# Loading k and v with four tokens on each of 128 partitions and the last 64 tokens apart

## The chip, the core and the metric

The kernel runs on one core of one Trainium2 chip. The metric is the device time of one execution in microseconds (us), as the median of several runs. A core has TensorE (PE, with PEld for its weight loads), VectorE (DVE), ScalarE (ACT), GpSimd (POOL) and SyncE (SP), and 16 DMA engines that move data between the device memory (HBM) and the on-chip memory (SBUF, 128 partitions). In this kernel SP issues every DMA, on one queue.

## The reference, cut to what matters

Inputs q, k and v have the shape (4, 8, 576, 64): batch, heads, tokens, head size, in float32. The first stage is an attention without softmax, the second and third are two feed-forward stages over the 2304 tokens.

```python
kv = np.einsum('bhsd,bhse->bhde', k, v)          # 64 x 64 for each batch and head: a sum over the 576 tokens
out = np.einsum('bhsd,bhde->bhse', q, kv)
x = out / np.sqrt(np.mean(out * out, axis=-1, keepdims=True) + 1e-06) * g_norm
x = x.transpose(0, 2, 1, 3).reshape(2304, 512)
h = np.maximum(np.maximum(x @ w1, x @ w2), x @ w3)
x = h @ w_out                                    # the first feed-forward stage
for e in range(4):                               # the second one, with p the normalized domain_probs
    y += p[:, e:e + 1] * (np.maximum(x @ e_w1[e], 0) @ e_w2[e])
```

The sum over tokens in kv may be taken in any order, as long as k and v put the same token in the same place.

## The kernel before, in words

All matrix products are done by PE in float32 or in split float32. The kernel has three stages, whose instructions are written out in one order for all engines; each engine takes its own in that order and waits for what an instruction needs.

The attention stage reads a string of steps (`steps`, from line 680). `K b c` (`att_kv`, line 261) forms kv of two heads of batch b from the tiles of k and v; each tile holds four heads, so the tile pair (b, c) serves `K b 2c` and `K b 2c+1`. Per head there are five products, one for each column i of the tile: four sum over 128 partitions, the last over the first 64. After the fourth K step of a batch, ACT copies kv into a padded operand (`kvb`). `T` (`att_T`) transposes a tile of q (line 297), `O` (`att_O`) multiplies it by kvb (lines 313 and 321) and squares the outcome (line 334), `N` (`att_N`) normalizes it on DVE, `X` (`att_X`) transposes it for the next stage (line 364, with a copy at 368 or 370). Between them stand the steps `a` and `b` (`conv_a`, `conv0`, `conv1`), which turn the weights of the first feed-forward stage from 64-bit words into float32 on ACT, POOL and DVE (lines 199 to 211), and `A`, `H`, `P`, the first products of that stage (lines 249 and 415). The steps end near 135 us in the profile; the two feed-forward stages follow, with the products at lines 537 and 577 as the bulk of the time.

The loads of q, k, v and of these weights are issued by SP in the order of the list `order` (line 637): k00 q0 k01 q1 q2 k10 k11 q3 q4 q6 k20 q5 k21 k30 k31, then three weight tiles, q8, q9 and further weights; each "k" entry is a call of `load_kv` and loads a tile of k and one of v. There are buffers for six tiles of k and v (three pairs) and six of q. `pump` emits the loads as far as buffers have been released by the steps emitted so far, and on the chip SP waits for that release.

A tile of k or v has 128 partitions, four heads, five columns and 64 values. In the kernel before, partitions 0 to 63 get five successive tokens each (tokens 0 to 319), partitions 64 to 127 four each (tokens 320 to 575), by one DMA for each half: 64 partitions x 4 heads packets of 1280 and of 1024 bytes. Tiles of q take two tokens for each partition and head, so packets of 512 bytes; the tile of the last 64 tokens of all batches (q2) comes as four DMAs of 32 partitions.

Of the kernel before, what the change touches and what calls it, by code (L numbers as in the profile page):

```python
# [21 lines left out]
def tile_attn_moe_moe2(  # L22
# [23 lines left out]
    nc = tc.nc  # L46
    B, H, S, D = q.shape
# [3 lines left out]
    P = 128  # L51
# [8 lines left out]
    KC = S // P  # L60
# [56 lines left out]
    for b0 in range(0, B, 2):  # L117
        for b, s0 in ((b0, 0), (b0, 256), (b0, None), (b0 + 1, 0), (b0 + 1, 256)):
# [3 lines left out]
            else:  # L122
                rows = out[b * S + s0 : b * S + s0 + 256, :].rearrange("(p r) d -> r p d", r=2)
# [20 lines left out]


    HALF = P // 2
    KS = HALF * (KC + 1)

    def load_kv(pool, b, c):
        for src, nm in ((k, "k"), (v, "v")):  # L150
            t = pool.tile([P, 4, KC + 1, D], F32, tag="kv", name=f"{nm}{b}_{c}", bufs=6)
            rows = src[b, 4 * c : 4 * c + 4]
            nc.sync.dma_start(out=t[0:HALF], in_=rows[:, 0:KS, :].rearrange("h (p c) d -> p h c d", c=KC + 1))
            nc.sync.dma_start(
                out=t[HALF:P, :, 0:KC, :], in_=rows[:, KS:S, :].rearrange("h (p c) d -> p h c d", c=KC)
            )
            kv_sb[nm, b, c] = t


# [246 lines left out]
    def moe1_h(pool, j, f, xs):  # L406
        for i in range(3):
            moe1_a(i, j, f, xs)
        return moe1_split(pool, j, f)
# [210 lines left out]
    with tc.manual_schedule():  # L620
# [114 lines left out]
        h = moe1_h(None, 2, 0, xs)  # L735
# [12 lines left out]
        for j in range(2, NB):  # L748
            acc = new_acc(KD)
            for f in range(NF):  # L750
                if j > 2 or f:
                    h = moe1_h(None, j, f, xs)
# [117 lines left out]
```

## Time and profile before

| | |
|---|---|
| median of 3 runs | 1159.07 us (1158.97 to 1159.13) |
| the profiled execution | 1160.35 us, span 1158.5 us |
| PE busy | 1123.4 us (97%) |
| PEld, the weight loads, beside PE | 1033.8 us (89%) |
| DVE busy | 562.4 us (49%) |
| ACT busy | 391.1 us (34%) |
| POOL busy | 238.1 us (21%) |
| DMA on the queue of SP | 98.62 MB in 73824 packets, 28.0% of the 16 engines' span |

The span runs from the first to the last instruction of the profiled execution; the rest of its time lies around that. A busy share is the mean over stages with different limits. A row of a timeline gives the start, the duration, the engine, the line in the kernel, the operation with what it writes and reads, and in brackets the idle time before it and what ended that; neighbouring instructions of one kind are merged. A DMA issue has a time to landing, from the start of its issue on SP until its data has arrived. A transfer's packet is one contiguous piece.

### The profile page before, as it was taken

The numbers are of one execution on the slowest core, as the hardware profiler recorded it, in microseconds if no ns is written. First come the engines' busy times: TensorE is split into PE (matmuls) and PEld (weight loads), VectorE is DVE, ScalarE is ACT, GpSimd is POOL, SyncE is SP. The second block draws the span as 40 slices with busy tenths as digits, with TensorE's granted clock in tenths as the row PEclk, the third lists the DMA queues.
The fourth block names the chain that finished last, engine by engine and source line by source line (L and its number), as shares of the span: only waits on it lengthen the run. The fifth ranks groups of instructions, "written<-read, shape, count | busy, mean of one in ns | idle before, by whom it ended". The sixth has DMA issues, their size and how long they took to land.

```text
span 1158.5 us, 15032 instructions
## 1 busy us (share of the span) xinstructions
PE 1123.4 (97%) x6096; PEld 1033.8 (89%) x6096; DVE 562.4 (49%) x842; ACT 391.1 (34%) x699; POOL 238.1 (21%) x178
## 2 busy tenths in 40 slices
PE   5699899999999999999999999999999999999998
PEld 5689799999999988888888888888888888888887
DVE  0689982221315544343753435583534666453523
ACT  2463331121214434243553233352323253332321
POOL 1156760000300130205220110512020522002000
PEclk9899999999999999999999999999999999999999
DMA  9963421000201220204250403424040625030111
GB/s 206 226 169 109 146 74 56 2 28 1 64 1 65 68 87 28 82 7 157 65 191 1 160 4 114 141 74 145 19 146 1 216 66 191 1 130 35 46 64 55
DMA packets 73894, 99.59 MB, mean 86 GB/s; under 512 B 6240, under 2 KB 49248, under 8 KB 73824
## 3 DMA queue, kind: packets, MB, share of 16 engines
q1 hardware_dynamic: 73824, 98.62, 28.0%
q8 instruction: 48, 0.79, 0.3%
q14 instruction: 22, 0.18, 0.0%
HBM read 75.01 MB, written 23.59 MB: 85 GB/s over the span
## 4 chain that ended last, share of the span: by engine, by line
PE 87%; DVE 5%; DMA 4%; SPq 2%; ACT 1%; issue 1%; POOL 1%; DVEq 0%; ACTq 0%
PE bank L577 35%; PE bank L537 30%; PE bank L249 15%; PE bank L415 6%; DMA k<-in_k_dram 2%; DMA stage_a<-in_moe_w_dram 1%; DVE cv_a L208 1%; DMA v<-in_v_dram 1%; DVE cv_a L211 1%; SPq L135 1%; DVE cv_a L207 0%; DVE fa L394 0%; PE bank L297 0%; SPq L611 0%; POOL cv_o L200 0%
## 5 line engine op out<-in xcount | busy, mean ns | idle before, releaser
L577 PE MATMUL bank<-wr,hr 128*128 128x512 f32 x792 | 227.1, 395 | 0.0
L561 DVE TENSOR_TENSOR fa<-bank,fa 128x384 f32<-128x384 f32 x144 | 80.2, 557 | 214.1 <-ACT fa L558 120.4
L577 PEld LDWEIGHTS bank<-wr,hr 128*128 128x128 f32 x792 | 147.0, 188 | 20.7
L519 POOL TENSOR_TENSOR fa<-fa 128x768 f32<-128x768 f32 x48 | 97.1, 2033 | 299.4 <-DMA fa<-y_d 221.6
L249 PE MATMUL bank<-xr,wr 128*128 128x384 f32 x792 | 145.2, 340 | 5.8 <-DVE fa L394 2.5
L249 PEld LDWEIGHTS bank<-xr,wr 128*128 128x128 f32 x792 | 139.6, 188 | 8.7 <-DVE fa L394 3.4
L488 POOL TENSOR_TENSOR w1s<-w1s 128x256 f32<-128x256 f32 x64 | 55.7, 890 | 421.6 <-DMA w1s<-in_moe_w_dram 420.4
L558 ACT ACTIVATE fa<-bank 128x384 f32<-128x384 f32 x144 | 70.7, 491 | 194.5 <-PE bank L537 194.5
L537 PE MATMUL bank<-rb,wr 128*128 128x384 f32 x648 | 131.6, 338 | 0.3 <-DVE hr L545 0.3
L537 PE MATMUL bank<-xr,wr 128*128 128x384 f32 x648 | 131.6, 338 | 0.0
L537 PEld LDWEIGHTS bank<-rb,wr 128*128 128x128 f32 x648 | 116.6, 188 | 10.2 <-DVE hr L545 0.6
L537 PEld LDWEIGHTS bank<-xr,wr 128*128 128x128 f32 x648 | 116.7, 188 | 9.6
L577 PE MATMUL bank<-wr,xr 128*128 128x512 f32 x324 | 100.8, 396 | 0.0
L394 DVE TENSOR_TENSOR fa<-bank,fa 128x384 f32<-128x384 f32 x72 | 39.8, 555 | 117.7 <-PE bank L249 117.5
L249 PE MATMUL bank<-xr,wl 128*128 128x384 f32 x504 | 90.5, 335 | 0.0
L249 PEld LDWEIGHTS bank<-xr,wl 128*128 128x128 f32 x504 | 87.4, 188 | 0.2 <-DVE wl L185 0.2
L577 PE MATMUL bank<-wl,hr 128*128 128x512 f32 x288 | 86.3, 394 | 0.0
L545 DVE SCALAR_TENSOR_TENSOR hr<-fa,hr 128x384 fp32r<-128x384 f32 x72 | 49.7, 690 | 42.6 <-ACT hr L544 42.6
L577 PEld LDWEIGHTS bank<-wr,xr 128*128 128x128 f32 x324 | 60.7, 188 | 10.8
L544 ACT ACTIVATE hr<-fa 128x384 fp32r<-128x384 f32 x72 | 37.8, 525 | 77.1 <-DVE fa L561 77.1
L577 PEld LDWEIGHTS bank<-wl,hr 128*128 128x128 f32 x288 | 53.4, 188 | 7.0
L544 ACT ACTIVATE xr<-fa 128x384 fp32r<-128x384 f32 x48 | 25.2, 525 | 96.7 <-DVE fa L561 96.7
(132 smaller groups left out, 1481.9 us busy)
## 6 DMA issues: line engine op xcount, KB each, us to landing
fa<-y_d SPq DMA_DIRECT2D x22, 768.0 KB, 6.4
stage_a<-in_moe_w_dram SPq DMA_DIRECT2D x18, 512.0 KB, 3.6
o_d<-fa SPq DMA_DIRECT2D x36, 256.0 KB, 3.7
fa<-o_d SPq DMA_DIRECT2D x36, 256.0 KB, 5.6
w1s<-in_moe_w_dram SPq DMA_DIRECT2D x32, 256.0 KB, 3.2
w2s<-in_moe_w_dram SPq DMA_DIRECT2D x32, 256.0 KB, 4.1
y_d<-fa SPq DMA_DIRECT2D x6, 768.0 KB, 3.8
o_d<-ob SPq DMA_DIRECT2D x18, 256.0 KB, 2.0
```

The source lines that it names most:

```text
L135: nc.sync.dma_start(out=t[bb * n : (bb + 1) * n], in_=q[bb, :, SB:S, :].rearrange("h (p r) d -> p h r d", r=2))
L249: nc.tensor.matmul(ps, w[:, wi, c * P : (c + 1) * P], x[xi][:, c, :], start=(n == 0), stop=(n == 3 * KD - 1),)
L394: nc.vector.tensor_tensor(out=ms[j, f], in0=ps[:, :T], in1=ms[j, f], op=ALU.max)
L415: nc.tensor.matmul(acc[c][:, :T], w[:, wi, c * P : (c + 1) * P], h[hi], start=(f == 0 and n == 0), stop=(f == NF - 1 and n == 2),)
L488: eng.tensor_tensor(out=st[:, o], in0=st[:, a], in1=st[:, b], op=ALU.subtract)
L519: eng.tensor_tensor(out=yb[:, o], in0=yb[:, a], in1=yb[:, b], op=op)
L537: nc.tensor.matmul(out, w[wi][:, c * P : (c + 1) * P], y[yi][:, c, :], start=(i == 0 and k in BEGIN), stop=(i == 5), skip_group_check=k no ...
L544: nc.scalar.activation(out=h[0], in_=src, func=AF.Relu)
L545: nc.vector.scalar_tensor_tensor(out=h[1], in0=src, scalar=0.0, in1=f32(h[0]), op0=ALU.max, op1=ALU.subtract)
L558: nc.scalar.activation(out=s[k // 2], in_=a, func=AF.Copy)
L561: nc.vector.tensor_tensor(out=t, in0=x, in1=t, op=ALU.add)
L577: nc.tensor.matmul(banks[i], h[a, i // TPB][hi][:, i % TPB * P : (i % TPB + 1) * P], w[a][wi], start=(pr == 0 and a == 0 and m == 0), stop ...
```

## The change

A tile keeps its shape, and the products are as before. The first DMA now fills all 128 partitions with four successive tokens each (tokens 0 to 511, `KS = P * KC`), 128 partitions x 4 heads packets of 1024 bytes. The second fills the fifth column of partitions 0 to 63 with one token each (tokens 512 to 575), 64 partitions x 4 heads packets of 256 bytes.

```diff
     HALF = P // 2
-    KS = HALF * (KC + 1)
+    KS = P * KC

     def load_kv(pool, b, c):
         for src, nm in ((k, "k"), (v, "v")):
             t = pool.tile([P, 4, KC + 1, D], F32, tag="kv", name=f"{nm}{b}_{c}", bufs=6)
             rows = src[b, 4 * c : 4 * c + 4]
-            nc.sync.dma_start(out=t[0:HALF], in_=rows[:, 0:KS, :].rearrange("h (p c) d -> p h c d", c=KC + 1))
-            nc.sync.dma_start(
-                out=t[HALF:P, :, 0:KC, :], in_=rows[:, KS:S, :].rearrange("h (p c) d -> p h c d", c=KC)
-            )
+            nc.sync.dma_start(out=t[:, :, 0:KC, :], in_=rows[:, 0:KS, :].rearrange("h (p c) d -> p h c d", c=KC))
+            nc.sync.dma_start(out=t[0:HALF, :, KC, :], in_=rows[:, KS:S, :].rearrange("h p d -> p h d"))
             kv_sb[nm, b, c] = t
```

## Rows read from the trace of the kernel before

**Rows 1.** The page, part 4: the chain that ended last, shares of the span by line.

```profile
PE bank L577 35%; PE bank L537 30%; PE bank L249 15%; PE bank L415 6%; DMA k<-in_k_dram 2%; DMA stage_a<-in_moe_w_dram 1%; DVE cv_a L208 1%; DMA v<-in_v_dram 1%; DVE cv_a L211 1%; SPq L135 1%; DVE cv_a L207 0%; DVE fa L394 0%; PE bank L297 0%; SPq L611 0%; POOL cv_o L200 0%
```

**Rows 2.** Stretches: width, busy us by engine, granted PE clock, DMA share, GB/s.

```profile
0.00:64.00 64.00, 42.66 (x461) 38.38 (x462) 24.46 (x54) 25.18 (x51) 12.10 (x13) 0.95 1.10 218
...
75.00:135.00 60.00, 56.40 (x334) 53.15 (x332) 57.67 (x93) 24.12 (x46) 40.03 (x28) 1.00 0.37 115
135.00:1158.00 1023.00, 1015.77 (x5205) 935.46 (x5204) 472.61 (x681) 333.91 (x588) 181.78 (x135) 1.00 0.22 75
```

**Rows 3.** The timeline of PE, 0 to 75 us.

```profile
9.04 1.53 PE L271 MATMUL bank<-v,k 128*64 128x64 f32 x20 [9.04 <-DMA v<-in_v_dram]
...
33.15 2.55 PE L271 MATMUL bank<-v,k 128*64 128x64 f32 x40 [3.84 <-DMA v<-in_v_dram]
...
48.02 1.09 PE L297 MATMUL bank<-ident,q 128*128 128x128 f32 x8 [2.03 <-DMA q<-in_q_dram]
...
53.46 2.41 PE L271 MATMUL bank<-v,k 128*64 128x64 f32 x40 [3.47 <-DMA v<-in_v_dram]
...
66.29 0.66 PE L364 MATMUL bank<-ident,xt 128*128 128x128 f32 x4 [0.22 <-DVE fa L370]
66.88 1.82 PE L271 MATMUL bank<-v,k 128*64 128x64 f32 x40
70.94 1.56 PE L297 MATMUL bank<-ident,q 128*128 128x128 f32 x8 [2.24 <-ACT s L344]
```

**Rows 4.** The timeline of SP's DMA issues, 42 to 66 us.

```profile
42.69 1.10 SPq L154 DMA_DIRECT2D v<-in_v_dram  x1
...
53.34 0.59 SPq L154 DMA_DIRECT2D v<-in_v_dram  x1
...
58.99 6.58 SPq L139 DMA_DIRECT2D q<-in_q_dram  x2
```

**Rows 5.** The DMA issued from 59 to 59.5 us: KB, us to landing.

```profile
q<-in_q_dram SPq DMA_DIRECT2D x1, 512.0 KB, 11.8
```

**Rows 6.** Stretches in which one kind of load moves (columns as in rows 2).

```profile
18.00:20.00 2.00, 2.00 (x24) 1.76 (x23) 0.00 (x0) 0.54 (x2) 0.00 (x0) 1.00 1.20 200
33.00:36.00 3.00, 2.85 (x42) 2.47 (x43) 1.95 (x6) 0.20 (x1) 0.00 (x0) 0.64 1.21 290
37.00:39.00 2.00, 2.00 (x24) 1.61 (x23) 0.69 (x1) 1.40 (x3) 0.00 (x0) 0.94 1.12 197
58.00:63.00 5.00, 5.00 (x59) 4.69 (x57) 3.92 (x4) 3.78 (x9) 3.16 (x1) 1.00 1.11 220
64.00:66.00 2.00, 2.00 (x30) 1.53 (x28) 1.90 (x4) 0.26 (x1) 0.00 (x0) 1.00 1.10 346
```

**Rows 7.** The second DMA of v21, issued from 42.6 to 42.8 us.

```profile
v<-in_v_dram SPq DMA_DIRECT2D x1, 256.0 KB, 10.6
```

**Rows 8.** The second DMA of v31, among those issued from 50 to 55 us.

```profile
v<-in_v_dram SPq DMA_DIRECT2D x1, 256.0 KB, 11.1
```

**Rows 9.** The timeline of SP, 200 to 420 us: the loads of p_all.

```profile
201.54 2.02 SPq L611 DMA_DIRECT2D p_all<-in_moe_domain_probs_dram  x4
```

**Rows 10.** The page, part 6: DMA issues, KB each, median us to landing.

```profile
p_all<-in_moe_domain_probs_dram SPq DMA_DIRECT2D x8, 4.0 KB, 1.9
```

**Rows 11.** Waits of SP's queue, 0 to 90 us: total, times, longest us.

```profile
SPq L154 <- DMA q<-in_q_dram: 2.9, 2, 2.0
SPq L153 <- DMA k<-in_k_dram: 1.8, 2, 0.9
```

**Rows 12.** The page, part 2: all DMA packets.

```profile
DMA packets 73894, 99.59 MB, mean 86 GB/s; under 512 B 6240, under 2 KB 49248, under 8 KB 73824
```

**Rows 13.** The timeline of ACT: the first conversion of a weight tile.

```profile
65.74 0.66 ACT L199 ACTIVATE cv_a<-stage_a 128x512 f32<-128x512 f32 x1 [2.22 <-DMA stage_a<-in_moe_w_dram]
```

**Rows 14.** The timeline of DVE, 58 to 76 us.

```profile
58.80 0.96 DVE L70 CAST xr<-fa 128x1536 fp32r<-128x1536 f32 x1 [5.71 <-ACT fa L368]
...
75.08 0.69 DVE L335 TENSOR_REDUCE ss<-xt 128x8 f32<-128x512 f32 x1 [1.86 <-ACT xt L334]
```

## The prediction

> **What bounds the kernel now.** I read four views, in this order: the chain of waits, the stretches, the timelines, and the rates of the loads. The chain that ended last gives TensorE (PE) nearly everything, and among the lines that are not PE the largest is the DMA that loads k, at 2%, with v and the weight stage behind it at 1% each [rows 1]. The stretches say where: from 135 us to the end PE is busy 1015.77 of 1023 us, and from 75 to 135 us PE is busy 56.40 and VectorE (DVE) 57.67 of 60; but in the first 64 us PE is busy only 42.66, with the 16 DMA engines at a share of 1.10, so occupied without a pause, at 218 GB/s [rows 2]. The loads of k, v and q therefore set the pace of the first 64 us, and the rest follows in a fixed order. PE's timeline shows the same from the other side: it starts at 9.04 us, when v has come, waits 3.84 us before 33.15 and 3.47 us before 53.46 for v, 2.03 us before 48.02 for q, and 2.24 us before 70.94 [rows 3]. The last of these is put down to ScalarE (ACT), but q8, issued at 58.99, lands 11.8 us later, at 70.8 [rows 4, 5]; both let go together.
>
> Last I asked how fast each kind of load moves while the queue is full [rows 6]: k and v in 64-partition transfers with packets of 1024 and 1280 B 220 GB/s (58 to 63 us); weights with 128 partitions and 1024 B packets 346 (64 to 66); q with 128 partitions and 512 B packets 290 (33 to 36); the four q2 transfers with 32 partitions each and 512 B packets 200 (18 to 20). A packet twice as large does not help k and v against q; the number of partitions in a transfer goes with the rate.
>
> **The change part by part.** Sixteen tiles (k and v, 4 batches, 2 halves of the heads) are loaded, each of 4 x 576 x 64 x 4 = 589,824 B. *Removed:* per tile a transfer of 327,680 B and one of 262,144 B, together 589,824 / 220,000 = 2.68 us, so 42.9 us of the first 64. The landings agree: v31's second transfer, issued at 53.34, lands at 64.4, that of v21, issued at 42.69, at 53.3; four tiles (k30, v30, k31, v31) lie between, 11.1 us or 2.8 each [rows 4, 7, 8].
>
> *Added, the main transfer:* 524,288 B on 128 partitions in 512 packets of 1024 B. No load of k or v in this form is in the trace. The nearest row is the weight stage, same bytes, partitions and packets: 524,288 / 346,000 = 1.52 us. The other end is q, at 290 GB/s (1.81 us) in one stretch but 197 (2.66 us) in another, where q6 of batch 2 moves [rows 6]. I take 1.52, keeping 2.66 as the far end.
>
> *Added, the tail:* 65,536 B on 64 partitions, 256 packets of 256 B, 16 for each DMA engine. Nothing before has such packets. From below: bytes at the 220 GB/s of 64 partitions, 0.30 us. From above: a q2 transfer has as many packets, each twice as large, and takes 131,072 / 200,000 = 0.66 us [rows 6]. Further off, the p_all transfers (128 packets of 32 B) are issued four in 2.02 us and land 1.9 us after issue, so they take no more than 0.51 us each, or 1.02 for 256 packets [rows 9, 10]. I take the middle of the two nearer ends, 0.48.
>
> [...] No row here shows a load of 256 B. [...]
>
> *Sum of the loads:* 1.52 + 0.48 = 2.00 us for a tile in place of 2.68; 16 x 0.68 = 10.9 us. The number of transfers stays two a tile, so SP's issues (0.6 us each when unhindered) and the transfers in flight stay as many; SP's longest waits here are for an earlier landing, of 2.0 us at most [rows 11], so it follows the faster queue. Packets rise by 16 x 256 = 4096, of 73,894 [rows 12].
>
> [...]
>
> **Does PE follow?** Landings move by 0.68 us for each tile ahead of them. v21 is the 12th tile: from 53.3 to 45.1, and the products waiting at 53.46 start near 45.3. From there PE has, at present, 15.2 us with no wait above a quarter microsecond, up to 66.88 + 1.82 = 68.70 [rows 3]: these would end at 60.5. [...] q8 has all 16 tiles ahead: 70.8 becomes 59.9. So the transposes of 70.94 start at 60.5 by PE and 59.9 by q8: a lead of 10.4 to 11. ACT's wait for the first weights (2.22 us before 65.74) also goes, since these land 10.9 us earlier [rows 13]. DVE's work from 58.80 to 75.08 hangs on the same products, and its last row there starts after a wait of 1.86 us for ACT, behind the transposes of 70.94 [rows 14]; it keeps the same lead. What is late next is that PE and DVE work itself.
>
> Matmuls, copies and their order are untouched: five products a head take the same 128 and 64 partitions, only holding other tokens. After 75 us nothing waits for a load of k, v or q: weights are issued when DVE frees a stage, so they move with it. A lead at 75 us should reach the end. The loads' 10.9 us is my term; profiled 1160.35 (span 1158.5 and 1.85 around it) becomes 1149.45. The median shown, 1159.07, is 1.28 lower: 1159.07 - 10.9 = 1148.2 us.
>
> **Rivals.** *Doubled rate:* twice the partitions move twice the 220 GB/s. Main is 524,288 / 440,000 = 1.19, a tile 1.67, the loads lose 16.2 us, but v21 only 12 x 1.01 = 12.1, and PE, which then no longer waits 2.24 us for q8, leads by at most 14.3: 1144.8. For it: the step from 200 with 32 partitions to 346 with 128; against: the 346 itself. *Slow tail:* a 256 B packet costs as much as one of 512 B to q2, 0.66 us a tail; a tile is 2.18 and the gain 8.0: 1151.1. For it: q's rate on 128 partitions is below that of the weights, whose packets are larger; against: k and v show no gain from larger packets. [...] *Slower k and v reads:* the rate depends on where the bytes lie, as 197 beside 290 GB/s for q hints. At 290 throughout a tile is 1.81 + 0.48 = 2.29 and the gain 6.2: 1152.8. If batch 2's four tiles run at 197 (3.14 us each) and the rest at 346, it is 12 x 0.68 - 4 x 0.46 = 6.3: 1152.8. For it: q6; against it: the four-tile landings above don't test it, being limited at 220. *No change:* tail packets cost what p_all's bound allows, 1.02 us; a tile is 2.54, the gain 2.2: 1156.9. The same verdict follows if DVE, at 57.67 of 60 us, absorbs the lead; against that, it has no work that is due at a fixed time. *Slower:* main at 197 for every tile with tail 0.66: 3.32 us, 16 x 0.64 = 10 lost: 1169. It decides from the point where main and tail exceed 2.68, with my tail a rate below 524,288 / 2.20 = 238 GB/s. For it: q6 shows that it can happen with 128 partitions; against: weights at 346 and q at 290 in the stretch before.
>
> **How the numbers follow.** Forecast, a gain of 9 to 13: 0.57. Doubled rate: 0.06. Slow tail: 0.10. Slower reads: 0.14. No change: 0.07. Slower: 0.06. About 0.2%, 2.3 us, is what a measurement can tell from none. With the tail at 0.30 the loads lose 0.86 x 16 = 13.8, and PE's lead is 12 x 0.86 + 0.6 + 2.24 = 13.2; the doubled rate with the 0.6 of clock reaches 14.9, so the low end is 1144. The high end, 1154, takes in the slow tail and the slower reads. Outside lie no change and slower, 0.13. Faster 0.87, same 0.07, slower 0.06.
>
> **What would show it.** The page should count 77,990 packets and the same bytes. In the stretches of k and v alone the rate should be near 590 KB / 2.00 = 295 GB/s, not 220. PE should start near 7 to 8 us, the waits before 33.15 and 53.46 should shrink, the last v land near 53.5 and the transposes of 70.94 start near 60.3; from there every row should be 10 to 11 us early, up to the end. Wrong would be: that rate below 250, a first product later than 9.04, or a lead at 75 us that is gone at 135.

## The result, and the profile after

The changed kernel takes 1148.12 us (median of 4 runs, 1146.83 to 1149.5) against 1159.02 for the kernel before on the same chip: a ratio of 0.9908, with a 95% interval of 0.9891 to 0.9925. That is 10.9 us less; 1148.2 was predicted. The profiled execution is the fastest of the four (1146.83, span 1145.0), while that of before lies 1.3 above its median. The two traces therefore differ by 13.5 us, 2.6 more than the medians, and the account below is that of the traces. (Lines of the changed kernel stand two earlier behind the loads: 269 for 271, 295 for 297.)

The page, part 2, counts the packets that were forecast, 77,990 [rows 12], and the same bytes:

```profile
DMA packets 77990, 99.59 MB, mean 87 GB/s; under 512 B 10336, under 2 KB 53344, under 8 KB 77920
```

The stretches of the changed kernel (width, busy us of PE, PEld, DVE, ACT and POOL, granted PE clock, DMA share, GB/s) answer to [rows 2, 6]:

```profile
0.00:64.00 64.00, 50.79 (x582) 45.56 (x583) 32.53 (x73) 34.66 (x71) 17.63 (x17) 0.97 1.03 256
...
44.00:50.00 6.00, 6.00 (x54) 5.81 (x53) 3.88 (x9) 4.31 (x9) 1.22 (x1) 0.72 1.14 264
48.00:52.00 4.00, 4.00 (x48) 3.70 (x48) 3.07 (x4) 2.67 (x6) 3.22 (x1) 1.00 1.12 258
53.00:55.00 2.00, 2.00 (x32) 1.74 (x30) 1.90 (x4) 1.52 (x4) 0.64 (x1) 1.00 1.10 346
```

In the same 64 us PE now does 8 us more work. From 48 to 52 us only k and v move, at 258 GB/s where it was 220; the weights still move at 346.

PE's timeline answers to [rows 3]:

```profile
7.56 1.53 PE L269 MATMUL bank<-v,k 128*64 128x64 f32 x20 [7.56 <-DMA v<-in_v_dram]
...
27.30 1.82 PE L269 MATMUL bank<-v,k 128*64 128x64 f32 x40 [1.46 <-DMA v<-in_v_dram]
...
39.16 1.09 PE L295 MATMUL bank<-ident,q 128*128 128x128 f32 x8
...
42.94 1.88 PE L269 MATMUL bank<-v,k 128*64 128x64 f32 x40 [1.81 <-DMA v<-in_v_dram]
...
56.00 1.82 PE L269 MATMUL bank<-v,k 128*64 128x64 f32 x40
59.03 1.07 PE L295 MATMUL bank<-ident,q 128*128 128x128 f32 x8 [1.21 <-DMA q<-in_q_dram]
...
63.69 2.34 PE L247 MATMUL bank<-xr,wl 128*128 128x384 f32 x12
```

Set against the rows of before, the lead grows step by step: 1.5 us at the first product, 5.9 at the one of 33.15, 8.9 at the transposes of 48.02, 10.5 at 53.46, 10.9 at 66.88 and 11.9 at the transposes of 70.94. The first product of the next stage is this row in the kernel before:

```profile
77.16 2.33 PE L249 MATMUL bank<-xr,wl 128*128 128x384 f32 x12
```

It leads by 13.5, and so does the end: from it to the end both take 1081.3 us (1158.5 - 77.16 and 1145.0 - 63.69). In these two profiles nothing was given back later.

The issues on SP, and below them the landing times of the same three transfers (v21's tail, v31's tail, q8), answer to [rows 4, 5, 7, 8]:

```profile
36.75 0.61 SPq L154 DMA_DIRECT2D v<-in_v_dram  x1
...
44.53 1.07 SPq L154 DMA_DIRECT2D v<-in_v_dram  x1
...
49.18 4.24 SPq L139 DMA_DIRECT2D q<-in_q_dram  x2
```

```profile
v<-in_v_dram SPq DMA_DIRECT2D x1, 64.0 KB, 6.5
...
v<-in_v_dram SPq DMA_DIRECT2D x1, 64.0 KB, 7.8
...
q<-in_q_dram SPq DMA_DIRECT2D x1, 512.0 KB, 9.7
```

v21 is complete at 43.2, v31 at 52.3, q8 at 58.9. Four tiles take 9.1 us, 2.28 each, in place of 11.1.

### The profile page after: what moved, and what is told of

It reads as the page before. It is cut to its first block, busy times and chain, and to the rows that moved or that the text cites. A ratio compares the mean times of both kernels' runs of the same rounds, so it can differ in the third digit from the quotient of the medians.

```text
span 1145.0 us, 15032 instructions
## 1 busy us (share of the span) xinstructions
PE 1120.5 (98%) x6096; PEld 1031.7 (90%) x6096; DVE 562.7 (49%) x842; ACT 390.9 (34%) x699; POOL 236.8 (21%) x178
## 2 busy tenths in 40 slices
DMA packets 77990, 99.59 MB, mean 87 GB/s; under 512 B 10336, under 2 KB 53344, under 8 KB 77920
## 4 chain that ended last, share of the span: by engine, by line
PE 88%; DVE 5%; DMA 2%; SPq 2%; ACT 1%; issue 1%; POOL 1%; DVEq 0%; ACTq 0%
PE bank L575 35%; PE bank L535 30%; PE bank L247 15%; PE bank L413 6%; DMA v<-in_v_dram 1%; DVE cv_a L206 1%; DVE cv_a L209 1%; PE bank L269 1%; DMA k<-in_k_dram 1%; PE bank L362 1%; DVE cv_a L205 1%; SPq L154 0%; PE bank L319 0%; DVE fa L392 0%; SPq L135 0%
## 5 line engine op out<-in xcount | busy, mean ns | idle before, releaser
L543 DVE SCALAR_TENSOR_TENSOR hr<-fa,hr 128x384 fp32r<-128x384 f32 x72 | 50.0, 695 | 42.6 <-ACT hr L542 42.6
```

Of the source, the lines that this page charges most:

```text
L543: nc.vector.scalar_tensor_tensor(out=h[1], in0=src, scalar=0.0, in1=f32(h[0]), op0=ALU.max, op1=ALU.subtract)
```

## The experiments

All ran against the kernel before on the same chip; diffs are against the changed kernel. The tile costs are read as above, from the landing of v21 to that of v31, four tiles later. Two profiles of the changed kernel differ by 0.13 us a tile in that window (last run), so where it matters a mean stands beside it, called the mean over the pairs: the k and v tiles of pairs 2 to 8, each pair from the landing before it to its own. For the changed kernel it is 2.16 us a tile in the first profile and 2.25 in the second.

**The main transfer as two halves.** Only the number of partitions that a transfer spans is undone.

```diff
-            nc.sync.dma_start(out=t[:, :, 0:KC, :], in_=rows[:, 0:KS, :].rearrange("h (p c) d -> p h c d", c=KC))
+            for n in range(2):
+                nc.sync.dma_start(
+                    out=t[n * HALF : (n + 1) * HALF, :, 0:KC, :],
+                    in_=rows[:, n * HALF * KC : (n + 1) * HALF * KC, :].rearrange("h (p c) d -> p h c d", c=KC),
+                )
```

> The changed kernel with its main transfer issued as two of 64 partitions each; token layout, packets of 1024 B and the tail stay. Theory 'partitions' (the partitions that one transfer spans set its rate): the main part goes back to 524,288 B at 220 GB/s = 2.38 us, a tile to 2.86 us in place of the 2.28 measured in the changed kernel, the stretch with k and v alone to 206 GB/s, and the time rises by 16 x 0.58 = 9 us to about 1157. Rival 'layout' (the gain comes from the even packets or the new token order): the stretch stays near 258 GB/s and the time near 1148.

1160.22 us, ratio to before 1.0006 (0.9996 to 1.0015): the whole gain is gone. The issues of the last transfers of v21 and v31, their landing times, and the stretch of k and v:

```profile
45.44 0.61 SPq L158 DMA_DIRECT2D v<-in_v_dram  x1
...
57.77 0.60 SPq L158 DMA_DIRECT2D v<-in_v_dram  x1
```

```profile
v<-in_v_dram SPq DMA_DIRECT2D x1, 64.0 KB, 8.3
...
v<-in_v_dram SPq DMA_DIRECT2D x1, 64.0 KB, 7.3
```

```profile
54.00:60.00 6.00, 6.00 (x62) 5.63 (x59) 1.97 (x4) 3.85 (x8) 0.05 (x1) 0.72 1.16 212
```

From 53.7 to 65.1 it is 11.3 us, 2.83 a tile, as the theory "partitions" had it, and 212 GB/s. (That the time is 3 us above the 1157 expected goes in part with q5, which takes 2.7 us again where the changed kernel takes 1.6; last section.) Token order and packets are those of the changed kernel, so they are not the cause. The run also has three transfers a tile where the changed kernel has two; but the kernel before has two as well, and takes 2.8.

**Without the tail.**

```diff
-            nc.sync.dma_start(out=t[0:HALF, :, KC, :], in_=rows[:, KS:S, :].rearrange("h p d -> p h d"))
...
-                nc.tensor.matmul(o, kt[0:n, hh, i, :], vt[0:n, hh, i, :], start=(i == 0), stop=(i == KC))
+                nc.tensor.matmul(o, kt[0:n, hh, i % KC, :], vt[0:n, hh, i % KC, :], start=(i == 0), stop=(i == KC))
```

> The tail transfer is left out, and the fifth product of each head reads column 0 again, so the sum lacks the last 64 tokens. Theory 'slow main' (main 1.80 us at 290 GB/s, tail 0.48): the stretch with k and v alone shows 290 GB/s and four tiles land in 7.2 us in place of 9.1. Rival 'dear tail' (main 1.52 us at 346 GB/s as I predicted, tail 0.76): 346 GB/s and 6.1 us. The time falls by 16 x 0.48 = 7.7 us to about 1140.5 if PE follows all the way; with PE's own chain as the limit by 5 us, to 1143.

1142.77 us, ratio 0.986 (0.9846 to 0.9875). The issues of v21 and v30, two tiles apart, and their landing times (k31 had to wait for a buffer and was issued at 37.15 only, so v31 doesn't serve):

```profile
28.57 1.42 SPq L153 DMA_DIRECT2D v<-in_v_dram  x1
...
31.33 1.09 SPq L153 DMA_DIRECT2D v<-in_v_dram  x1
```

```profile
v<-in_v_dram SPq DMA_DIRECT2D x1, 512.0 KB, 7.8
...
v<-in_v_dram SPq DMA_DIRECT2D x1, 512.0 KB, 8.0
```

From 36.4 to 39.3 it is 2.96 us for two: the main transfer alone takes 1.48, or 354 GB/s. My 1.52 was right for it, and by this window the tail costs 2.28 - 1.48 = 0.80 us (0.67 with the 2.15 of the changed kernel's second profile). The mean over the pairs, here pairs 2 to 7, is 1.58, which puts the tail at 0.58 to 0.67. The time fell by 5.4 us rather than 16 x 0.80 = 12.8, or 16 x 0.6 = 9.6: the transposes of the eighth q tile start at 52.70, 6.3 us earlier than in the changed kernel, since PE by then waits for little (it is busy 5.00 of the 5.00 us from 34 to 39). What the tail still costs the kernel is thus 5.4 us.

**Each tail twice.**

```diff
             nc.sync.dma_start(out=t[0:HALF, :, KC, :], in_=rows[:, KS:S, :].rearrange("h p d -> p h d"))
+            spare = pool.tile([HALF, 4, D], F32, tag="spare", name=f"s{nm}{b}_{c}", bufs=6)
+            nc.sync.dma_start(out=spare, in_=rows[:, KS:S, :].rearrange("h p d -> p h d"))
```

> Each tail is loaded a second time, into a buffer that nobody reads. Theory 'slow main' (tail 0.48 us): a tile takes 2.76 us, four tiles land in 11.0 us, and the time rises by 16 x 0.48 = 7.7 us to 1156. Rival 'dear tail' (0.76 us): 3.04 us, 12.2 us for four tiles, and 12 us more, 1160. If the tail hides beside the main transfer it costs nothing and the time stays at 1148.

1157.96 us, ratio 0.9993 (0.9981 to 1.0006), 9.8 us above the changed kernel, between what the two theories gave. The spare tails of v21 and v31:

```profile
45.31 0.61 SPq L156 DMA_DIRECT2D sv<-in_v_dram  x1
...
56.53 0.61 SPq L156 DMA_DIRECT2D sv<-in_v_dram  x1
```

```profile
sv<-in_v_dram SPq DMA_DIRECT2D x1, 64.0 KB, 6.5
...
sv<-in_v_dram SPq DMA_DIRECT2D x1, 64.0 KB, 6.3
```

Four tiles take 11.0 us, 2.75 each: by this window the second tail costs 0.47, the 0.48 that I had taken, and the first 0.80. I took the difference for a loss of 0.33 that comes only where a tail is set between main transfers, and the three runs that follow ask what it is. The traces do not bear the split: with the second profile's 2.15 the second tail costs 0.60 and the first 0.67, and by the means over the pairs (2.81 here) the second costs 0.56 to 0.65 and the first 0.58 to 0.67. First and second tail cost alike, about 0.6 us, midway between the 0.48 and 0.76 of the two theories.

**Both tails behind both main transfers.** Within `load_kv` the tails of k and v are issued in a second loop, after the main transfers of both.

> Of each pair the two main transfers are issued first, then both tails; bytes and packets as in the changed kernel. So far: the main transfer takes 1.48 us where no tails stand between, a tile with a tail 2.28, a second tail 0.47 more. Theory 'change of form' (about 0.33 us are lost where a transfer of 128 partitions meets one of 64, the tail itself takes 0.47): a pair takes 2 x 1.48 + 2 x 0.47 + 0.33 = 4.23 us in place of 4.56, the loads end 8 x 0.33 = 2.6 us sooner, 1145.5. Rival 'a first read is dear' (a tail costs 0.80, and the second tail of that run was cheap as it read the same bytes again): a pair stays at 4.56 us and the time at 1148.

1147.79 us, ratio 0.9908 (0.989 to 0.9926), as the changed kernel. v's tails of the two pairs:

```profile
36.29 0.61 SPq L158 DMA_DIRECT2D v<-in_v_dram  x1
...
44.88 1.03 SPq L158 DMA_DIRECT2D v<-in_v_dram  x1
```

```profile
v<-in_v_dram SPq DMA_DIRECT2D x1, 64.0 KB, 6.7
...
v<-in_v_dram SPq DMA_DIRECT2D x1, 64.0 KB, 7.2
```

From 43.0 to 52.1: 9.1 us for four tiles, as in the changed kernel's first profile, where the theory "change of form" gave 8.5; the mean over the pairs is 2.20. Half as many changes of form cost as much, so that theory gets no support. The 9.1 is what the rival "a first read is dear" gave, but a second tail that costs as much as the first speaks against that one.

**The tail as 512 B packets on 32 partitions.**

```diff
-            nc.sync.dma_start(out=t[0:HALF, :, KC, :], in_=rows[:, KS:S, :].rearrange("h p d -> p h d"))
+            nc.sync.dma_start(
+                out=t[0 : HALF // 2, :, KC : KC + 2, :],
+                in_=rows[:, KS:S, :].rearrange("h (p c) d -> p h c d", c=2),
+            )
```

The tile gets a sixth column, and the last two products of a head run over 32 partitions.

> The tail as two tokens on each of 32 partitions, 128 packets of 512 B in place of 256 of 256 B; each head takes a sixth product, over 32 partitions, 64 products more. Theory 'packets' (a tail's cost goes with its packets): it halves, 0.24 to 0.40 us a tile, the loads end 6 us sooner, and with some of the products on the way 1143 to 1145. Rival 'bytes to few partitions' (the q2 rate of 200 GB/s or less for 32 partitions): 0.33 us of its own and the same loss around it, a gain of 2 us at most, eaten by the products: 1147 to 1149.

1147.21 us, ratio 0.9896 (0.9881 to 0.9911). The tails of v21 and v31:

```profile
34.91 0.72 SPq L154 DMA_DIRECT2D v<-in_v_dram  x1
...
42.73 1.38 SPq L154 DMA_DIRECT2D v<-in_v_dram  x1
```

```profile
v<-in_v_dram SPq DMA_DIRECT2D x1, 64.0 KB, 6.5
...
v<-in_v_dram SPq DMA_DIRECT2D x1, 64.0 KB, 6.5
```

From 41.4 to 49.2 it is 7.8 us, 1.95 a tile: about 0.47 above the bare main transfer (by the mean over the pairs 2.04, or 0.46 above), where the tail of 256 B packets cost 0.58 to 0.80. In this one profile the same bytes are cheaper in half the packets. The transposes of the eighth q tile start at 56.39, 2.6 us before those of the changed kernel, but the first product of the next stage only 1.9 (61.76), and the span is 1144.8, so that nearly all of it is given back after that; what takes it back was not followed.

**One tail transfer for all heads of a batch.** The tails of k and of v go to tiles of their own, 64 partitions with 8 heads, issued before the four main transfers of the batch; packets stay at 256 B.

```diff
+        if c == 0:
+            for src, nm in ((k, "k"), (v, "v")):
+                t = pool.tile([HALF, H, D], F32, tag="tail", name=f"{nm}t{b}", bufs=4)
+                nc.sync.dma_start(out=t, in_=src[b, :, KS:S, :].rearrange("h p d -> p h d"))
+                tails[nm, b] = t
```

> The tails of all eight heads of a batch come in one transfer for k and one for v, ahead of the batch's four main transfers: 8 tail transfers of 128 KB in place of 16 of 64. Theory 'change of form': per batch 4 x 1.48 + 4 x 0.47 + 0.33 = 8.13 us in place of 9.12, the loads end 4 us sooner, 1144; the first product starts later, by up to 0.9 us, since both tails of batch 0 come first. Rival 'a first read is dear' or 'packets': 9.12 us stay, 1148 to 1149.

1148.68 us, ratio 0.9909 (0.9892 to 0.9925). The last main transfers of batches 2 and 3:

```profile
34.26 1.41 SPq L160 DMA_DIRECT2D v<-in_v_dram  x1
...
42.41 0.58 SPq L160 DMA_DIRECT2D v<-in_v_dram  x1
```

```profile
v<-in_v_dram SPq DMA_DIRECT2D x1, 512.0 KB, 8.4
...
v<-in_v_dram SPq DMA_DIRECT2D x1, 512.0 KB, 7.9
```

From 42.7 to 50.3 it is 7.6 us for the last batch, below even the 8.13 of the theory "change of form": 4 x 1.48 and 1.7 for 256 KB of tails. (Batch 2 took 8.5 with q5 left out; the changed kernel 8.9 and 9.2.) But the first product starts at 8.03 rather than 7.56, the products of batch 2 still wait 1.86 us before 42.79, and the time does not move.

So a tile with a tail of its own in 256 B packets takes 2.15 to 2.28 us in two orders, and with 512 B packets, or with one tail transfer for the batch (7.6 / 4), 1.9 to 1.95. That the tail's form matters is seen in one profile of each. No theory on record covers all three runs: the batch run has as many packets as the changed kernel and is cheaper. The cause stays open.

**All tokens on 96 partitions.** One transfer a tile, six tokens a partition, six products over 96 partitions.

```diff
-            nc.sync.dma_start(out=t[:, :, 0:KC, :], in_=rows[:, 0:KS, :].rearrange("h (p c) d -> p h c d", c=KC))
-            nc.sync.dma_start(out=t[0:HALF, :, KC, :], in_=rows[:, KS:S, :].rearrange("h p d -> p h d"))
+            nc.sync.dma_start(out=t[0:KP], in_=rows.rearrange("h (p c) d -> p h c d", c=KN))
```

> All 576 tokens come with one transfer on 96 partitions, six tokens and 1536 B a packet; each head takes six products over 96 partitions in place of five, 64 products more in all, some 3 us of PE. If the halves of the partitions have separate ways, the first half carries two thirds of the bytes at 220 GB/s: 393,216 / 220,000 = 1.79 us a tile, 330 GB/s, a gain over the changed kernel of up to 16 x 0.49 = 7.8 us, less about 3: 1143. If 96 partitions do no better than 290 GB/s: 2.03 us, gain 4 less 3: 1147. If anything under 128 partitions falls to 220 GB/s: 2.68 us, 1156 or more.

1154.93 us, ratio 0.9966 (0.9956 to 0.9976). v21 and v31:

```profile
35.33 2.01 SPq L154 DMA_DIRECT2D v<-in_v_dram  x1
...
46.71 0.48 SPq L154 DMA_DIRECT2D v<-in_v_dram  x1
```

```profile
v<-in_v_dram SPq DMA_DIRECT2D x1, 576.0 KB, 14.1
...
v<-in_v_dram SPq DMA_DIRECT2D x1, 576.0 KB, 13.3
```

From 49.4 to 60.0 it is 10.6 us, 2.65 a tile, 223 GB/s: the rate of 64 partitions (220), with the longest packets of all (1536 B) and the fewest transfers. The first tiles of the same run were faster. k01 and v01, issued at 2.20 and 3.14:

```profile
k<-in_k_dram SPq DMA_DIRECT2D x1, 576.0 KB, 10.0
...
v<-in_v_dram SPq DMA_DIRECT2D x1, 576.0 KB, 11.3
```

From 12.2 to 14.4 it is 2.24 us for v01, 263 GB/s, where the kernel before takes 2.75 for the same tile. So 223 is not a fixed rate of 96 partitions; what slows the later tiles stays open.

**The changed kernel once more.**

> The changed kernel once more, for a second profile. Its first profile had a span of 1145.0 us and other runs 1146.2 to 1147.7. Theory 'clock behind a pause': from the transposes of the eighth q tile to the first product of the next stage the kernel before takes 6.22 us with the granted clock low and the changed one 4.66 with it full; in a profile with a span of 1146.5 or more this stretch takes 6.2 us again, and the rest up to the end differs by less than 1 us. Rival: the spread sits elsewhere, as in the loads, and the stretch stays at 4.7.

1148.0 us, ratio 0.9903 (0.9888 to 0.9918). The profile's span is 1145.8, below the 1146.5 for which the theory spoke; the stretch is 4.65 us (59.12 to 63.77). So it says nothing on the spread of some 2.5 us between the runs of one kernel, which stays open. It does repeat the lead: 11.8 us at the transposes of the eighth q tile. A little of it is given back here: from the first product of the next stage to the end it is 1082.0 us, 0.7 more than in the first profile. The tails of v21 and v31:

```profile
38.28 0.61 SPq L154 DMA_DIRECT2D v<-in_v_dram  x1
...
45.06 1.14 SPq L154 DMA_DIRECT2D v<-in_v_dram  x1
```

```profile
v<-in_v_dram SPq DMA_DIRECT2D x1, 64.0 KB, 5.8
...
v<-in_v_dram SPq DMA_DIRECT2D x1, 64.0 KB, 7.6
```

From 44.1 to 52.7 it is 8.6 us, 2.15 a tile, where the first profile gave 2.28, and 276 GB/s from 48 to 52 us where that gave 258. The mean over the pairs goes the other way, 2.25 against 2.16. One window of one profile thus fixes a tile's cost to no better than some 0.1 us.

No version clearly beats the changed kernel: 1147.21 and 1147.79 against 1148.0 on the same chip are closer than their runs scatter.

## Why the prediction was right, point by point

- *The loads set the pace of the first 64 us, and the partitions in a transfer set their rate.* Shown: with the halves alone restored, the stretch of k and v goes from 258 to 212 GB/s and the time is that of before (ratio 1.0006).
- *Main transfer 1.52 us, from the weights' 346 GB/s.* Right: 1.48 to 1.58 without tails. *Tail 0.48.* Too low: about 0.6 (0.58 to 0.67 by the means over the pairs, 0.80 in the window of the first profile). *Their sum, 2.00.* Mis-sized: a tile takes 2.15 to 2.28, and the stretch 258 and 276 GB/s in the two profiles where 295 was forecast. That is the tile of the rivals "slow tail" (2.18) and "slower reads" (2.29), which gave 1151 to 1153; that the time is 1148 all the same has the reasons below. The middle of two bounds from transfers of other forms could not price the tail.
- *16 x 0.68 = 10.9 us from the loads.* The size came out for another reason than the one given. v31's landing moved from 64.4 to 52.3, by 12.1 us in these traces. The k and v tiles gave 9.4 of it: the eight pairs, each from the landing before it to its own, took 1.0, 1.1, 1.4, 2.1, 0.9, 0.7, 1.0 and 1.1 us less. q5 and q6 gave 3.0, which the sum left as they were, and the other loads took some 0.2 more. The two errors cancel, so that 1148.1 meets 1148.2 this closely is luck. The rival "slower reads" rested on q6's 197 GB/s, which I took for a matter of where the bytes lie; the same bytes land in 1.74 us in the changed kernel, 301 GB/s, so that hint was misread (last section).
- *PE follows.* It did, by a little more than forecast: the products of 53.46 start at 42.94 (forecast 45.3), right behind v21's main transfer, which lands at 42.8, and 0.3 us ahead of its tail. The prediction let them wait for the whole tile, but of a head's five products only the fifth, on 64 partitions, reads the tail. Where a tail is late, it waits alone, as for v10 in the second profile:

```profile
23.82 0.48 PE L269 MATMUL bank<-v,k 64*64 64x64 f32 x4 [0.96 <-DMA v<-in_v_dram]
```

  The transposes of 70.94 start right behind q8 (58.9), as forecast (59.9 and 60.5; measured 59.03). Faster loads than these gain less: with 512 B tails (and 64 more products) v31 lands 3.1 us sooner and the median differs by 0.8 us, without tails 8.9 us sooner and it differs by 5.4. With the 512 B tails PE's waits from 55 us on hold none for q8 (1.21 us in the changed kernel), so its own chain sets the pace there, the limit that the prediction named for faster loads; for the run without tails I take the same, an estimate from the busy 34 to 39 us.
- *The clock, 0.6 us in the low end of the range.* The 0.6 was an estimate of mine, 2.41 less 1.82 [rows 3], and no run shows it as what a shorter pause is worth. In its place the traces show this: the products of 53.46 took 1.88 us in place of 2.41, but the low clock now falls on 44 to 50 us (0.72), behind the wait of 1.81, and up to the end of the products of 66.88 PE's chain is shorter by 0.4 only (42.94 to 57.82, before 53.46 to 68.70). The prediction had nothing for a second place. From the transposes of 70.94 to the first product of the next stage the kernel before takes 6.22 us. PE had stood idle for 2.24 us, and the row below has a granted clock of 0.57:

```profile
71.00:75.00 4.00, 4.00 (x28) 3.34 (x29) 2.02 (x6) 2.81 (x5) 1.26 (x2) 0.57 0.42 138
```

  After a pause of 1.21 the changed kernel takes 4.66, at a granted clock of 1.00 from 59 to 64 us. These 1.6 us are the difference between the lead of 11.9 us and the 13.5 of the spans.
- *A lead at 75 us reaches the end.* Shown: from the first product of the next stage it is 1081.3 us in both. In the second profile of the changed kernel 0.7 of 13.4 us is lost on that way.

## What to carry to other kernels

Before splitting a load by partitions, sort the loads of a saturated stretch by how many partitions one transfer spans, and read GB/s from stretches with one kind each: that single table gave this result, while packet sizes alone pointed the other way: 220 GB/s with 1024 and 1280 B, 290 with 512 B [rows 6]. A small extra transfer has to be priced by runs with and without it, over many tiles and in more than one profile: the tail was put at 0.48 us and cost about 0.6, and windows of four tiles gave anything from 0.47 to 0.80. And when a rate is lower for one transfer than for its like, look also at what moves next to it (q5 took 3.1 and 1.6 us with the same data).

## What the runs showed of the hardware that I had not expected

Some q transfers of 128 partitions took longer in the runs whose tiles of k and v come on 64 or 96 partitions. In the kernel before, v20's second transfer and q5 are issued and land as follows (45.0 and 48.0):

```profile
35.81 0.61 SPq L154 DMA_DIRECT2D v<-in_v_dram  x1
36.47 1.27 SPq L139 DMA_DIRECT2D q<-in_q_dram  x1
```

```profile
v<-in_v_dram SPq DMA_DIRECT2D x1, 256.0 KB, 9.1
...
q<-in_q_dram SPq DMA_DIRECT2D x1, 512.0 KB, 11.5
```

That is 3.1 us for q5. It is 2.7 with the halves (45.5 to 48.2) and 2.8 with 96 partitions (41.6 to 44.4), but 1.6 in the changed kernel (37.1 to 38.7), 1.8 without tails and with tails twice. q6 takes 3.3 us in the kernel before (36.4 to 39.7) and 1.7 in the changed one (31.0 to 32.7). Data and place are the same in all; the neighbours differ. That they are the cause was not shown: q0, which stands between such tiles too, takes no more than 2.0 us in the kernel before, and 1.6 in the changed one.

In the last tiles 96 partitions move no faster than 64, 223 GB/s beside 220. I had expected up to 330 (an estimate: two thirds of the bytes at the 220 of 64 partitions); measured were 263 in the first tiles and those 223 in the last. For 128 partitions the most seen here is 354.
